# Attention with inducing points and a top-1 expert layer on one core: logits in column tiles, weights spread by a matmul, one gather per batch, and new numbers in the planner

## The chip, the cores and the metric

The kernel runs on one core of one Trainium2 chip. The metric is device time in microseconds (us): the median over runs of the program. The profile is of one execution.

## The reference, cut to what matters

```python
# x: (4, 11456, 128), inducing: (32, 128); 8 experts of width 1024; all fp32
def mab(q, kv):
    s = scale * (q @ kv.transpose(0, 2, 1)); s = s - s.max(-1, keepdims=True)
    a = np.exp(s); a /= a.sum(-1, keepdims=True) + 1e-09
    return a @ kv
h = mab(I, x)            # pass 1: 32 inducing points attend to 11456 rows
y = mab(x, h)            # pass 2: each row attends to the 32 rows of h
logits = y @ w_gate; expert_idx = np.argmax(logits, axis=1)
probs = softmax(logits); gate_w = probs[arange, expert_idx]
for e in range(E):       # the rows of expert e
    out[mask] = gate_w[mask, None] * (np.maximum(y[mask] @ w1[e], 0) @ w2[e])
```

## The kernel before, in words

Each of the four batches has six groups (24 in all), each of 4 segments by 15 blocks of 32 rows. A group's x lies in SBUF with channels on partitions (an xT tile, 0.98 MB); pass 1 needs it with rows on partitions as well: either loaded a second time (an xn load, 0.99 MB) or made on chip by 15 transposes on TensorE and four evictions (a group in `TURNED`). All big tiles (xT, xn and the output tiles ob) share 17 buffers; the 8 PSUM banks are shared too.

**Pass 1**, per group: scores S1 (`scores`, L445, four matmuls in four column tiles), maximum M1, exp E1, 32x32 block transposes T1, and the sum H (`h_sum`, L498). After six groups: the rows h, centred h (`h_center`), and `gate_mm`, `pick`: which expert all rows of the batch are expected to choose, from the mean of h. POOL then gathers the 128 rows of that expert's w1 (GA1) and of its w2 (GA2) by two indirect DMAs of 0.5 MB (`gather`, L549). From w1 come the hidden units G (`units`, L588, on TensorE), from those and w2 a 32x128 matrix h4 (`second`, L610, `part_fold`, L622), and a threshold (`extremes`, `margin`, `margin_all`, `threshold`) above which a row's choice is certain.

**Pass 2**, per group: scores S2 against centred h, M2 (`max2`), E2 (`exp2`). Then by rounds of one to four groups: LG (`logits`, L666), one 128x128 by 480 matmul for each group, all accumulating into one bank, where `gzb` puts group u's logits in its own columns; LV (`logits_turn`); the gate: RS, LS on POOL, PR on ACT, LM, GE, DN, C. C gives a weight for each row. For each group then CB (`spread`, L720, a DVE transpose that spreads the weights over the 32 points), W (`weigh`, L723, on POOL: e times cb), X (`experts`, L727, four matmuls in four row tiles, each to its own bank), four evictions V (L464 on ACT or L466 on DVE) into ob, and the store OUT (L439). At the end `count_left` (op LEFT) counts rows without a certain choice and, if there are any, a general part redoes them.

**The order** is made on the host by `schedule` (L59): it simulates the five engines with the planner's durations and due times, at each moment starts the ready op of lowest rank on each engine, and the instructions are written out in that order. On the chip each engine runs its own instructions strictly in that order, so an instruction whose input is late holds up all behind it. Ranks are `ONE`, `TWO` (a base and a step for each batch), `EARLY` for loads. A gather is planned to be done `GATHER` = 3600 ns after its 1100 ns issue:

```python
if o.dma:
    line = max(line, t + d + 500) + o.dma
    if e == "SP":
        o.end = line + LANDING
    ...
    else:
        o.end = t + d + GATHER
```

Of the kernel before, what the change touches and what calls it, by code (L numbers as in the profile page):

```python
# [18 lines left out]
P = 128  # L19
# [4 lines left out]
GB = 15  # L24
# [11 lines left out]
HOP, LANDING, INFLIGHT, GATHER, BEHIND = 70, 1400, 4, 3600, 450  # L36
# [21 lines left out]

def schedule(ops, caps, groups):  # L59
# [16 lines left out]
    line = inflight = t = done = 0  # L76

# [19 lines left out]
    while done < len(ops):  # L97
        for e in ENGINES:
# [25 lines left out]
            if o.dma:  # L124
                line = max(line, t + d + 500) + o.dma
                if e == "SP":
                    o.end = line + LANDING
                    inflight += 1
                    at(line, 1, o)
                else:  # L130
                    o.end = t + d + GATHER
# [25 lines left out]
D_S, D_H, D_X, D_LG, D_T4 = 830, 830, 860, 850, 440  # L157
PE_LAT = 180
# [9 lines left out]
ONE = ((-13.0, 0.5), (21.6, 0.8), (52.7, 3.0), (87.0, 3.4))  # L168
TWO = ((28.9, 6.3), (85.7, 4.0), (71.5, 10.3), (153.7, 6.2))
EARLY = 26.0  # L170
# [11 lines left out]
def make_plan(K):  # L182
# [3 lines left out]
    def op(name, rank, dur, fn, deps=(), take=(), use=(), lat=0, dma=0):  # L186
        if "PE" in dur and not lat:
            lat = PE_LAT
        o = Op(name, rank, dur, fn, deps, take, use, lat, dma)
        ops.append(o)  # L190
        return o

    prev_m = [None] * B
    xts, e2s = {}, {}
    chain = {}
    done_ops = []
    xt_free = {}
    for b in range(B):
# [5 lines left out]
        for g in range(NG):  # L204
# [4 lines left out]
            ld = op(f"LT{k}", r - EARLY, {"SP": 60}, lambda xt=xt[g], b=b, g=g: K.load_xt(xt, b, g), take=[xt[g]], dma=BYTES)  # L209
            xt_free[k] = ld  # L210
            fe = Buf("fe")
            s1[g] = op(f"S1.{k}", r, {"PE": D_S}, lambda fe=fe, xt=xt[g]: K.scores(fe, K.it_s, xt), [ld], take=[fe], use=[xt[g]])
            m1[g] = op(f"M1.{k}", r + 1, {"DVE": 625}, lambda fe=fe, b=b, g=g: K.max1(fe, b, g), [s1[g]], use=[fe])
            if g in TURNED[b]:
                xr = []
                on = op(f"ON{k}", r + .1, {"POOL": 125}, lambda xn=xn[g]: K.ones_col(xn), [ld], take=[xn[g]])
                for n, k0 in enumerate(range(0, GB, 4)):
                    m = min(4, GB - k0)
                    o = Buf("o")
                    tr = op(f"TR{k}.{n}", r + .2 + .2 * n, {"PE": 110 * m}, lambda o=o, xt=xt[g], k0=k0, m=m: K.turn(o, xt, k0, m), [ld, on], take=[o], use=[xt[g]])  # L220
                    w = m * 128
                    xr.append(op(f"TE{k}.{n}", r + .8 + .2 * n, {"ACT": 80 + int(.99 * w), "DVE": 75 + int(1.19 * w)}, lambda e, o=o, xn=xn[g], k0=k0, m=m: K.turn_out(e, o, xn, k0, m), [tr, on], use=[o, xn[g]]))
                xnr = xr
            else:
                xnr = [op(f"LN{k}", r - EARLY + 1, {"SP": 60}, lambda xn=xn[g], b=b, g=g: K.load_xn(xn, b, g), take=[xn[g]], dma=BYTES)]
            e1b, e1t = Buf("e1"), Buf("e1t")
            e1[g] = (fe, e1b, e1t, xnr)
            if g % 2:
                p = g // 2
                mi = Buf("mi")  # L230
                mq = op(f"MQ{b}.{p}", r + 1.5, {"DVE": 130}, lambda b=b, p=p: K.max_spread(b, p), [m1[g - 1], m1[g], nb_prev])
                fd = op(f"FD{b}.{p}", r + 1.6, {"PE": 220}, lambda mi=mi, b=b, p=p: K.max_fold(mi, b, p), [mq], take=[mi])
# [31 lines left out]
        gz = op(f"gz{b}", r + .5, {"DVE": 560}, lambda b=b: K.gate_cols(b), [a])  # L264
        gzb = op(f"gb{b}", r + .6, {"POOL": 1100}, lambda b=b: K.gate_block(b), [gz])
        m0 = Buf("mi")
        a = op(f"G{b}", r + 1, {"PE": 560}, lambda mi=m0, w=w, b=b: K.units(mi, w, b), [ga1, hT], take=[m0], use=[w])
        gt = op(f"GT{b}", r + 1, {"DVE": 440}, lambda mi=m0, b=b: K.units_turn(mi, b), [a], use=[m0])
        gs = op(f"GS{b}", r + 1, {"DVE": 420}, lambda b=b: K.units_sum(b), [gt])
        gl = op(f"GL{b}", r + 1, {"DVE": 600}, lambda b=b: K.units_keep(b), [gs])  # L270
        m0 = Buf("mi")
        a = op(f"P{b}", r + 1, {"PE": 560}, lambda mi=m0, w=w, b=b: K.second(mi, w, b), [gl, ga2], take=[m0], use=[w])
        a = op(f"PC{b}", r + 1, {"ACT": 280, "DVE": 280}, lambda e, mi=m0, b=b: K.part_out(e, mi, b), [a], use=[m0])
        m0 = Buf("mi")
        a = op(f"PF{b}", r + 1, {"PE": 360}, lambda mi=m0, b=b: K.part_fold(mi, b), [a], take=[m0])
        h4 = op(f"h4{b}", r + 1, {"ACT": 280, "DVE": 280}, lambda e, mi=m0, b=b: K.h4_out(e, mi, b), [a], use=[m0])
        a = op(f"dx{b}", r + 2, {"DVE": 840}, lambda b=b: K.extremes(b), [gl])
        a = op(f"dm{b}", r + 2, {"DVE": 1200}, lambda b=b: K.margin(b), [a])
        m0 = Buf("mi")
        a = op(f"DF{b}", r + 2, {"PE": 360}, lambda mi=m0, b=b: K.margin_all(mi, b), [a], take=[m0])  # L280
# [3 lines left out]
        for n in ROUNDS[b]:  # L284
            lg, lv, gate = Buf("mi"), Buf("lv"), Buf("gate")
            lgs = []
            rr = rank2(b * NG + g0 + n - 1)
            e2 = {}
            for u in range(n):
# [5 lines left out]
                s = op(f"S2.{k}", r, {"PE": D_S}, lambda fe=fe, xt=xt[g], b=b: K.scores(fe, K.hc[b], xt), [hc], take=[fe], use=[fe, xt[g]])  # L295
                mm = op(f"M2.{k}", r + 1, {"DVE": 780}, lambda fe=fe, k=k: K.max2(fe, k), [s], use=[fe])
                ex = op(f"E2.{k}", r + 2, {"ACT": 605}, lambda fe=fe, e=e2[u], k=k: K.exp2(fe, e, k), [mm], take=[e2[u]], use=[fe])
                lgs.append(op(f"LG{k}", rr + 2.7, {"PE": D_LG}, lambda lg=lg, e=e2[u], b=b, u=u, n=n: K.logits(lg, e, b, u, n), [ex, gzb, *lgs], take=[lg] if not u else [], use=[lg, e2[u]]))
            lt = op(f"LV{k}", rr + 3.6, {"DVE": 670}, lambda lg=lg, lv=lv: K.logits_turn(lg, lv), lgs[-1:], take=[lv], use=[lg])
            rs = op(f"RS{k}", rr + 3.7, {"DVE": 560}, lambda lv=lv, gt=gate, n=n: K.gate_rs(lv, gt, n), [lt], take=[gate], use=[lv])  # L300
            ls = op(f"LS{k}", rr + 3.8, {"POOL": 730}, lambda lv=lv, gt=gate, n=n: K.gate_ls(lv, gt, n), [rs], use=[lv, gate])
# [25 lines left out]
class Issue:  # L327
# [225 lines left out]
    def gather1(self, w, b):  # L553
        self.gather(self.w[w.slot][0], self.w1, b)
# [487 lines left out]
```

## Time and profile before

| | us |
|---|---|
| median of 3 runs | 205.47 (204.34 to 206.66) |
| profiled execution, its own time | 206.1 |
| its span, first to last instruction | 204.3 |
| busy PE / DVE / ACT / POOL | 162.1 / 132.0 / 95.9 / 56.9 |
| mean granted TensorE clock | 0.925 |
| bytes moved by DMA | 65.81 MB, 322 GB/s over the span |

PE is TensorE's matmuls, PEld its weight loads, DVE VectorE, ACT ScalarE, POOL GpSimd, SP the engine that issues loads and stores. Lines such as L588 are of the kernel before. A chain of waits is followed back from the last instruction: at each step to what released it. Granted clock is a share of full speed: TensorE has two levels, 2.4 and 1.2 GHz, so 0.5 is the lower one throughout.

### The profile page before, as it was taken

How to read it: one execution, taken by the hardware profiler on the slowest of the kernel's cores; microseconds unless marked ns; L12 is line 12 of the kernel's file. 1: busy time of each engine (PE TensorE's matmuls, PEld its weight loads, DVE VectorE, ACT ScalarE, POOL GpSimd, SP SyncE). 2: the span in 40 equal slices, each digit the busy share in tenths (PEclk: the TensorE clock that was granted, in tenths of full speed). 3: DMA queues.
4: the chain of work that ended last, by engine and by line, in shares of the span. 5: the costliest groups of instructions: out<-in, count | busy, mean ns of one | idle time of the engine just before them, and what ended most of it. 6: DMA issues, size and time to landing. Idle time of an engine off the chain costs nothing.

```text
span 204.3 us, 4408 instructions
## 1 busy us (share of the span) xinstructions
PE 162.1 (79%) x1664; PEld 83.3 (41%) x1665; DVE 132.0 (65%) x375; ACT 95.9 (47%) x197; POOL 56.9 (28%) x91
## 2 busy tenths in 40 slices
PE   0599999673999799379997999199999969983900
PEld 0274866353343357144224954026553223341300
DVE  1125737961579899746669889186998985997500
ACT  2056561071033663705635483307777725767630
POOL 0000000230003734710024635202373740397200
PEclk9999999996799999969999999969999988998585
DMA  6999999999997089999879899944058898179792
GB/s 206 419 423 424 415 424 409 423 408 421 413 410 290 3 262 365 397 423 390 316 311 349 308 418 348 415 178 189 6 241 325 288 374 332 75 313 385 290 404 94
DMA packets 10541, 65.81 MB, mean 322 GB/s; under 512 B 1424, under 2 KB 1552, under 8 KB 10512
## 3 DMA queue, kind: packets, MB, share of 16 engines
q1 hardware_dynamic: 8928, 61.06, 75.2%
q0 software_dynamic: 1152, 4.19, 5.6%
q8 instruction: 15, 0.25, 0.5%
q10 hardware_dynamic: 432, 0.20, 0.3%
q14 instruction: 14, 0.11, 0.2%
HBM read 41.85 MB, written 23.59 MB: 320 GB/s over the span
## 4 chain that ended last, share of the span: by engine, by line
PE 46%; DMA 21%; DVE 18%; ACT 4%; issue 3%; POOL 2%; ACTq 0%; DVEq 0%; POOLq 0%
DMA w1r<-in_w,ii 17%; PE bank L445 11%; PE bank L727 8%; PE bank L666 8%; PE bank L498 7%; PE bank L456 7%; DMA csb<-in_consts 4%; ACT big L464 2%; DVE e1t L488 2%; POOL e L723 2%; DVE mx L659 2%; PE bank L588 2%; DVE cb L720 2%; ACT e L485 1%; DVE mx L448 1%
## 5 line engine op out<-in xcount | busy, mean ns | idle before, releaser
L464 ACT COPY big<-bank 128x480 f32<-128x480 f32 (+2 forms) x121 | 60.4, 580 | 40.5 <-PE bank L727 22.8
L723 POOL TENSOR_TENSOR e<-e,cb 128x480 f32<-128x480 f32 x24 | 28.6, 1210 | 33.5 <-DVE cb L720 21.7
L727 PE MATMUL bank<-e,h 32*128 32x480 f32 x192 | 32.2, 691 | 1.9 <-POOL e L723 1.9
L445 PE MATMUL bank<-big,it_s 128*32 128x480 f32 x192 | 26.8, 615 | 6.4 <-DVE it_s L409 6.4
L498 PE MATMUL bank<-big,e1t 128*32 128x129 f32 x720 | 28.3, 287 | 1.9 <-DVE mq L471 1.6
L498 PEld LDWEIGHTS bank<-big,e1t 128*32 128x32 f32 x720 | 23.7, 115 | 10.1 <-issue 3.4
L663 ACT ACTIVATE e<-bank,nb 128x480 f32<-128x480 f32 x24 | 15.8, 671 | 24.2 <-DVE nb L660 12.0
L666 PE MATMUL bank<-e,gzb 128*128 128x480 f32 x48 | 26.7, 646 | 0.0
L445 PE MATMUL bank<-big,hc 128*32 128x480 f32 x192 | 25.7, 592 | 0.0
L448 DVE TENSOR_REDUCE mx<-bank 128x1 f32<-128x480 f32 x24 | 15.3, 643 | 11.3 <-PE bank L445 11.3
L456 PE MATMUL bank<-csb,big 128*128 128x128 f32 x150 | 20.4, 291 | 0.9 <-DMA csb<-in_consts 0.9
L686 POOL TENSOR_TENSOR ls<-lv,rs 128x315 f32<-128x315 f32 (+3 forms) x9 | 6.1, 678 | 53.4 <-DVE rs L683 48.8
L485 ACT ACTIVATE e<-bank,mx 128x480 f32<-128x480 f32 x24 | 14.9, 667 | 12.4 <-DVE mx L482 12.3
L456 PEld LDWEIGHTS bank<-csb,big 128*128 128x128 f32 x150 | 18.0, 151 | 6.3 <-DMA csb<-in_consts 2.5
L727 PEld LDWEIGHTS bank<-e,h 32*128 32x128 f32 x192 | 11.6, 208 | 15.3 <-issue 6.1
L488 DVE STREAM_TRANSPOSE e1t<-e 128x480 f32<-128x480 f32 x24 | 15.1, 653 | 2.0 <-ACT e L485 2.0
L659 DVE TENSOR_REDUCE mx<-bank 128x1 f32<-128x480 f32 x24 | 15.3, 638 | 1.3 <-PE bank L445 1.3
L720 DVE STREAM_TRANSPOSE cb<-c 128x480 f32<-128x480 f32 x24 | 15.3, 660 | 1.1 <-POOL e L723 0.9
L588 PE MATMUL bank<-w1r,hT_all 128*32 128x256 f32 x32 | 3.6, 523 | 15.1 <-DMA w1r<-in_w,ii 15.1
L466 DVE COPY big<-bank 128x480 f32<-128x480 f32 (+2 forms) x15 | 9.4, 627 | 8.8 <-PE bank L456 6.2
L666 PEld LDWEIGHTS bank<-e,gzb 128*128 128x128 f32 x48 | 7.9, 204 | 15.5 <-issue 10.8
L445 PEld LDWEIGHTS bank<-big,it_s 128*32 128x32 f32 x192 | 5.8, 113 | 14.0 <-DVE it_s L409 6.1
(94 smaller groups left out, 142.2 us busy)
## 6 DMA issues: line engine op xcount, KB each, us to landing
big<-in_xT SPq DMA_DIRECT2D x24, 960.0 KB, 11.6
out<-big SPq DMA_DIRECT2D x24, 960.0 KB, 4.8
big<-in_xn SPq DMA_DIRECT2D x14, 967.5 KB, 11.4
csb<-in_consts ACTq DMA_DIRECT2D x1, 172.5 KB, 7.9
w1r<-in_w,ii POOLq DMA_INDIRECT x4, 9.7
w2r<-in_w,ii POOLq DMA_INDIRECT x4, 9.9
it_s<-in_indT ACTq DMA_DIRECT2D x1, 16.0 KB, 5.4
wg_sb<-in_wg ACTq DMA_DIRECT2D x1, 4.0 KB, 9.8
```

What stands on the lines that cost most here:

```text
L445: self.nc.tensor.matmul(self.blk(ps[32 * q : 32 * q + 32, :GW]), lhsT=lhsT, rhs=x[:, :, q, :], start=True, stop=True)
L448: self.nc.vector.tensor_reduce(self.mx1[b][g // 2][:, g % 2 : g % 2 + 1], self.bank(fe)[:, :GW], AX.X, ALU.max)
L456: self.nc.tensor.transpose(ps[:, k * P : (k + 1) * P], x[:, k0 + k].rearrange("p q t -> p (q t)"), self.ident)
L464: self.nc.scalar.copy(dst, src)
L485: self.nc.scalar.activation(self.at(e), self.bank(fe)[:, :GW], AF.Exp, bias=self.mx1[b][p + 1][:, 2:3])
L488: self.nc.vector.transpose(self.at(t), self.at(e))
L498: self.nc.tensor.matmul(ps[32 * j : 32 * j + 32, : P + 1], lhsT=e[:, k, :], rhs=x[:, k, :], start=(n < 4), stop=(n >= 2 * GB - 4))
L659: self.nc.vector.tensor_reduce(t, self.bank(fe)[:, :GW], AX.X, ALU.max)
L666: self.nc.tensor.matmul(self.bank(lg)[:, :GW], lhsT=self.gzb[b][:, u].rearrange("p q s -> p (q s)"), rhs=self.at(e), start=(u == 0), stop= ...
L720: self.nc.vector.transpose(self.blk(self.at(cb)), c)
L723: self.nc.gpsimd.tensor_tensor(out=self.at(e), in0=self.at(e), in1=self.at(cb), op=ALU.mult)
L727: self.nc.tensor.matmul(self.bank(os_[q])[:, :GW], lhsT=self.h4[b][32 * q : 32 * q + 32, :], rhs=self.at(e)[32 * q : 32 * q + 32, :], star ...
```

## The change

- **Logits.** `gzb` shrinks from four 128x128 blocks to one 128x32 block. A round's LG is one op: n matmuls of 128x32, group u in column tile u, so the logits of group u stand on partitions 32u to 32u+31. All gate ops of a round work on 32n partitions and 60 columns instead of 128 partitions and 15n columns. LM, GE and DN go; C applies the threshold itself.
- **Weights.** Instead of a CB for each group: one DVE transpose CT (`gate_back`) for each round, then for each pair of groups SP (`spread`, "SEL" below): a matmul for each group, 32 rows of a 0/1 matrix `sel` against 480 columns, to a PSUM bank `cb`. W runs on DVE and reads that bank. `cb` buffers move from SBUF to the 8 shared banks.
- **Gather.** w1 and w2 lie side by side in one array `wcat`; one indirect DMA of 1 MB per batch replaces two.
- **Planner.** New durations; a gather is due 9030 ns after its start (1080+1500+700+2x2500+750) if the planned DMA line is busy, 6530 ns if not; a model of TensorE's clock; 8 planned loads in flight for 4; new ranks; `EARLY` 26 to 209.3. `ROUNDS` go from 9 to 10, turned groups from 10 to 9 (so one xn load more).
- **Smaller.** inducing points and constants are loaded on SP's queue, the latter behind the first xT; part of the threshold's work moves to POOL; `gate_mm` starts before centred h; the last two groups are stored in halves; LEFT reduces one array `c_all`.

```diff
-HOP, LANDING, INFLIGHT, GATHER, BEHIND = 70, 1400, 4, 3600, 450
+HOP, BEHIND = 55, 500
+FETCH, LANDING, INFLIGHT = 1500, 750, 8
[...]
...
+            if e == "PE":
+                d *= clock.speed(t)
+                clock.add(t, t + d)
...
-                line = max(line, t + d + 500) + o.dma
+                queued = line > t + d + FETCH
+                line = max(line, t + d + FETCH) + o.dma
...
-                    o.end = t + d + GATHER
+                    o.end = t + d + FETCH + 700 + (2 * o.dma if queued else o.dma) + LANDING
...
-TURNED = {0: (0, 1, 2, 3, 4), 1: (3,), 2: (3,), 3: (0, 1, 4)}
-
-ROUNDS = {0: (3, 3), 1: (4, 2), 2: (4, 2), 3: (3, 2, 1)}
-CAPS = {"e1": 3, "e1t": 4, "e2": 7, "cb": 2, "lv": 2, "gate": 2, "w": 1}
-GROUPS = {"bank": (8, {"fe": 3, "o": 5, "mi": 3}), "big": (17, {"xt": 10, "xn": 4, "ob": 4})}
...
+TURNED = {0: (0, 1, 2, 3, 5), 1: (3,), 2: (2,), 3: (0, 4)}
+
+ROUNDS = {0: (2, 2, 2), 1: (4, 2), 2: (2, 4), 3: (1, 4, 1)}
+
+HALVES = (22, 23)
+CAPS = {"e1": 3, "e1t": 4, "e2": 8, "lv": 3, "gate": 2, "w": 1}
+GROUPS = {"bank": (8, {"fe": 3, "o": 5, "mi": 3, "cb": 2}), "big": (17, {"xt": 10, "xn": 4, "ob": 4})}
...
-        ga1 = op(f"GA1.{b}", r, {"POOL": 1100}, lambda w=w, b=b: K.gather1(w, b), [a], take=[w], dma=1250)
-        ga2 = op(f"GA2.{b}", r, {"POOL": 1000}, lambda w=w, b=b: K.gather2(w, b), [a, ga1], use=[w], dma=1250)
...
+        ga = op(f"GA{b}", r, {"POOL": 1080}, lambda w=w, b=b: K.gather(w, b), [ix], take=[w], dma=2500)
...
+            a = op(f"C{k}", rr + 4.2, {"DVE": 1350}, lambda gt=gate, n=n, b=b, nr=nr: K.gate_c(gt, n, b, nr), [a, thr], use=[gate])
+            ct = op(f"CT{k}", rr + 4.3, {"DVE": 590}, lambda lv=lv, n=n, nr=nr: K.gate_back(lv, n, nr), [a], use=[lv])
+            rounds.append(ct)
+            for u0 in range(0, n, 2):
+                us = range(u0, min(u0 + 2, n))
+                cbs = [Buf("cb") for _ in us]
+                sp = op(f"SP{b * NG + g0 + u0}", rr + 4.4 + u0, {"PE": D["SEL"]}, lambda cbs=cbs, lv=lv, u0=u0: K.spread(cbs, lv, u0), [ct, sel], take=cbs, use=[lv])
+                for u, cb in zip(us, cbs):
...
+                    wg = op(f"W{k}", ru + .1, {"DVE": 650}, lambda cb=cb, e=e2[u]: K.weigh(cb, e), [sp], use=[cb, e2[u]])
...
+                    step = 2 if k in HALVES else 4
...
+    def logits(self, lg, es, b):
+        for u, e in enumerate(es):
+            self.nc.tensor.matmul(
+                self.bank(lg)[32 * u : 32 * u + 32, :GW], lhsT=self.gzb[b].rearrange("p q j -> p (q j)"), rhs=self.at(e), start=True, stop=True
+            )
...
+    def gate_back(self, lv, n, r):
+        self.nc.vector.transpose(self.lv4(lv, n), self.c_all[0 : 32 * n, r].unsqueeze(3).to_broadcast([32 * n, GB, NQ, E]))
+
+    def spread(self, cbs, lv, u0):
+        for i, cb in enumerate(cbs):
+            rows = slice(32 * (u0 + i), 32 * (u0 + i) + 32)
+            self.nc.tensor.matmul(
+                self.bank(cb)[:, :GW], lhsT=self.sel[rows].rearrange("p q m -> p (q m)"), rhs=self.at(lv)[rows], start=True, stop=True
+            )
...
-        self.nc.gpsimd.tensor_tensor(out=self.at(e), in0=self.at(e), in1=self.at(cb), op=ALU.mult)
+        self.nc.vector.tensor_tensor(out=self.at(e), in0=self.at(e), in1=self.bank(cb)[:, :GW], op=ALU.mult)
...
-        nc.vector.memset(self.done[64:128, :, NBLK - 1 : NBLK], 1.0)
-        nc.vector.tensor_scalar(self.left, self.done.rearrange("p b n -> p (b n)"), -1.0, 1.0, op0=ALU.mult, op1=ALU.add)
-        nc.vector.tensor_reduce(self.cnt, self.left, AX.X, ALU.add)
+        nc.vector.tensor_reduce(self.cnt[:, 0:1], self.c_all.rearrange("p r k q -> p (r k q)"), AX.X, ALU.min)
+        nc.vector.tensor_single_scalar(self.cnt[:, 1:2], self.cnt[:, 0:1], 0.0, op=ALU.is_le)
```

## Rows read from the trace of the kernel before

**Rows 1.** The profile's page: span, busy time by engine, and the span in 40 slices of 5.1 us (tenths of busy time, for PE and for the mean of the 16 DMA engines).

```profile
span 204.3 us, 4408 instructions
PE 162.1 (79%) x1664; PEld 83.3 (41%) x1665; DVE 132.0 (65%) x375; ACT 95.9 (47%) x197; POOL 56.9 (28%) x91
...
PE   0599999673999799379997999199999969983900
...
DMA  6999999999997089999879899944058898179792
```

**Rows 2.** The page's chain that ended last, by line, in shares of the span.

```profile
DMA w1r<-in_w,ii 17%; PE bank L445 11%; PE bank L727 8%; PE bank L666 8%; PE bank L498 7%; PE bank L456 7%; DMA csb<-in_consts 4%; ACT big L464 2%; DVE e1t L488 2%; POOL e L723 2%; DVE mx L659 2%; PE bank L588 2%; DVE cb L720 2%; ACT e L485 1%; DVE mx L448 1%
```

**Rows 3.** What TensorE's matmuls waited for, over the whole span: us in total, times, longest.

```profile
PE bank L588 <- DMA w1r<-in_w,ii: 15.1, 4, 4.7
PE bank L445 <- DVE it_s L409: 6.4, 1, 6.4
PE bank L744 <- DVE cnt L742: 3.6, 1, 3.6
PE bank L727 <- POOL e L723: 1.9, 2, 1.2
```

**Rows 4.** The chain in order of time (start, length): the four first gathers, from POOL's start to landing.

```profile
39.46 9.48 DMA w1r<-in_w,ii
...
78.37 9.85 DMA w1r<-in_w,ii
...
122.19 9.85 DMA w1r<-in_w,ii
...
158.83 6.06 DMA w1r<-in_w,ii
```

**Rows 5.** Stretches of the span: busy us of PE, PEld, DVE, ACT, POOL (with instructions), granted clock, DMA share, GB/s. The first four begin where G starts after its gather; the fifth is the end; the sixth holds half of the rounds.

```profile
49.00:56.00 7.00, 6.92 (x57) 3.35 (x58) 3.50 (x14) 0.00 (x0) 0.00 (x0) 0.64 1.02 417
88.30:92.40 4.10, 4.05 (x50) 2.57 (x54) 2.74 (x10) 0.00 (x0) 0.00 (x0) 0.60 1.01 423
132.10:136.30 4.20, 4.12 (x22) 1.21 (x22) 3.00 (x12) 0.00 (x0) 0.00 (x0) 0.59 0.69 286
165.00:170.30 5.30, 5.27 (x24) 1.50 (x25) 4.23 (x16) 1.75 (x4) 1.99 (x2) 0.68 0.95 363
184.00:194.20 10.20, 6.57 (x30) 2.42 (x26) 6.58 (x17) 6.82 (x16) 4.88 (x8) 0.67 0.84 344
140.00:190.00 50.00, 43.92 (x374) 19.49 (x376) 42.19 (x121) 32.08 (x70) 25.17 (x36) 0.94 0.68 267
```

**Rows 6.** The chain in order of time, whole ops of TensorE while the clock was at its upper level: 15 transposes of a group, two scores back to back, and one X, one group's LG, one scores (each logical fp32 matmul has two records).

```profile
13.78 1.79 PE bank L456 x15
...
92.39 1.75 PE bank L445 x16
...
98.38 1.02 PE bank L727 x8
99.39 1.00 PE bank L666 x2
100.40 0.94 PE bank L445 x8
```

**Rows 7.** Groups of instructions by shape (busy us, mean ns), and then, from the timeline (start, length), two gate ops of the last round, which has one group.

```profile
L723 POOL TENSOR_TENSOR e<-e,cb 128x480 f32<-128x480 f32 x24 | 28.6, 1210 | 33.5 <-DVE cb L720 21.7 <-ACT e L485 9.4 <-PE bank L727 2.2
L720 DVE STREAM_TRANSPOSE cb<-c 128x480 f32<-128x480 f32 x24 | 15.3, 660 | 1.1 <-POOL e L723 0.9
L466 DVE COPY big<-bank 128x480 f32<-128x480 f32 x10 | 6.5, 648 | 2.6 <-PE bank L727 2.4
L686 POOL TENSOR_TENSOR ls<-lv,rs 128x420 f32<-128x420 f32 x2 | 1.8, 922 | 19.2 <-DVE rs L683 19.2
L712 DVE TENSOR_REDUCE se<-ls 128x60 f32<-128x420 f32 x2 | 1.1, 564 | 0.0
L683 DVE RECIPROCAL rs<-sm 128x60 f32<-128x60 f32 x2 | 1.1, 528 | 0.1
...
184.08 0.38 POOL L686 TENSOR_TENSOR ls<-lv,rs 128x105 f32<-128x105 f32 x1
...
189.31 0.25 DVE L714 RECIPROCAL se<-se 128x15 f32<-128x15 f32 x1
```

**Rows 8.** The third batch's two gathers on POOL's timeline (start, length of the issue), and the page's line for the second gathers (median us from issue to landing).

```profile
122.19 1.06 POOL L549 DMA_INDIRECT w1r<-in_w,ii  x1 [2.46 <-DVE m L563]
...
124.49 0.99 POOL L549 DMA_INDIRECT w2r<-in_w,ii  x1 [0.16 <-issue]
...
w2r<-in_w,ii POOLq DMA_INDIRECT x4, 9.9
```

**Rows 9.** The end: the chain in order of time (start, length), and the last wait of SP's queue.

```profile
186.61 0.84 DVE left L741
187.47 0.54 DVE cnt L742
...
188.14 0.56 PE bank L744 x2
188.70 5.27 PE bank L727 x23
...
SPq L1037 <- DMA out<-big: 4.9, 1, 4.9
```

More of the change, by code (lines that the diff above doesn't have):

```diff
@@ L56, in __init__, with speed, add @@
             b.users += 1
+class Clock:
+    def __init__(self):
+        self.busy, self.fast = {}, {0: True}
+    def speed(self, t):
+        w = max(0, (t - PHASE) // WINDOW + 1)
+        for i in range(max(self.fast) + 1, w + 1):
+            self.fast[i] = self.busy.get(i - 1, 0) >= AWAKE[0 if self.fast[i - 1] else 1] * WINDOW
+        return 1 if self.fast[w] else 2
+    def add(self, t, end):
+        while t < end:
+            w = max(0, (t - PHASE) // WINDOW + 1)
+            stop = min(end, PHASE + w * WINDOW)
+            self.busy[w] = self.busy.get(w, 0) + stop - t
+            t = stop
 def schedule(ops, caps, groups):
@@ L76, in schedule @@
     line = inflight = t = done = 0
+    clock = Clock()
     def at(when, what, o):
@@ L184, in make_plan, with op @@
     ops = []
-    def op(name, rank, dur, fn, deps=(), take=(), use=(), lat=0, dma=0):
-        if "PE" in dur and not lat:
-            lat = PE_LAT
+    def op(name, rank, dur, fn, deps=(), take=(), use=(), lat=None, dma=0):
+        if lat is None:
+            lat = LAT.get(next(iter(dur)), 0)
         o = Op(name, rank, dur, fn, deps, take, use, lat, dma)
@@ L191, in op @@
         return o
[L193 to L197, printed above, removed]
+    xts, rounds = {}, []
+    it = op("IT", -1000, {"SP": 400}, lambda: K.load_it(), dma=60)
+    it = op("IS", -1000, {"DVE": 100}, lambda: K.scale_it(), [it])
+    cs = op("CS", rank1(0, 0) - EARLY + .01, {"SP": 400}, lambda: K.load_consts(), dma=500)
+    sel = op("SL", 20, {"POOL": 300}, lambda: K.make_sel(), [cs])
     for b in range(B):
@@ L294, in make_plan @@
                 e2[u] = Buf("e2")
[L295 to L298, printed above, removed]
@@ L308, in make_plan @@
[L308 to L320 removed]
+                s = op(f"S2.{k}", r, {"PE": D["S"]}, lambda fe=fe, xt=xt[g], b=b: K.scores(fe, K.hc[b], xt), [hc], take=[fe], use=[fe, xt[g]])
@@ new lines, in make_plan @@
+                mm = op(f"M2.{k}", r + 1, {"DVE": 800}, lambda fe=fe, k=k: K.max2(fe, k), [s], use=[fe])
+                exs.append(op(f"E2.{k}", r + 2, {"ACT": 550}, lambda fe=fe, e=e2[u], k=k: K.exp2(fe, e, k), [mm], take=[e2[u]], use=[fe]))
+            es = [e2[u] for u in range(n)]
+            a = op(f"LG{k}", rr + 2.7, {"PE": D["LG"]}, lambda lg=lg, es=es, b=b: K.logits(lg, es, b), [gzb, *exs], take=[lg], use=[lg, *es])
+            a = op(f"LV{k}", rr + 3.6, {"DVE": 600}, lambda lg=lg, lv=lv, n=n: K.logits_turn(lg, lv, n), [a], take=[lv], use=[lg])
@@ new lines, in make_plan @@
+            a = op(f"RS{k}", rr + 3.7, {"DVE": 700}, lambda lv=lv, gt=gate, n=n: K.gate_rs(lv, gt, n), [a], take=[gate], use=[lv])
+            a = op(f"LS{k}", rr + 3.8, {"POOL": 920}, lambda lv=lv, gt=gate, n=n: K.gate_ls(lv, gt, n), [a], use=[lv, gate])
+            a = op(f"PR{k}", rr + 3.9, {"ACT": 480}, lambda gt=gate, n=n: K.gate_exp(gt, n), [a], use=[gate])
+            a = op(f"C{k}", rr + 4.2, {"DVE": 1350}, lambda gt=gate, n=n, b=b, nr=nr: K.gate_c(gt, n, b, nr), [a, thr], use=[gate])
@@ L321, in make_plan @@
             g0 += n
     m0 = Buf("mi")
-    op("LEFT", 1e3, {"DVE": 1800}, lambda: K.count_left(m0), done_ops, take=[m0])
+    op("LEFT", 1e3, {"DVE": 900}, lambda: K.count_left(m0), rounds, take=[m0])
     return ops
@@ L350, in __init__ @@
         self.hT = new("hT_all", [P, B, P])
-        self.done = new("done_all", [P, B, NBLK])
-        self.left = new("left", [P, B * NBLK])
-        self.cnt = new("cnt", [P, 1])
+        self.rounds = sum(map(len, ROUNDS.values()))
+        self.c_all = new("c_all", [P, self.rounds, GB, NQ])
+        self.cnt = new("cnt", [P, 2])
         self.nleft = new("nleft", [P, 1], I32)
-        self.load = [lambda: nc.scalar.dma_start(self.it_s, indT), lambda: nc.scalar.dma_start(csb, consts), lambda: nc.scalar.dma_start(self.wg, wg)]
         self.pool = pool
@@ L759, in attn_moe_kernel @@
                 o.fn()
-    general_part(tc, K, xT, wg, w1, w2, out)
+    general_part(tc, K, xT, wg, wcat, out)
 def blk(t):
```

363 lines of the change are left out of this document (185 added, 178 removed).

## The prediction, made before the change was run

> **What bounds the kernel now.** I read the page first, then TensorE's waits, then the chain in order of time, and last the stretches that the chain points at. The page shows two resources that are near full for long stretches and neither over the whole span: PE is busy 162.1 of 204.3 us, the DMA engines are full to about 60 us and then in pieces [rows 1]. 65.81 MB at the 417 to 423 GB/s of a full stretch [rows 5] would take 157 us. So neither a byte nor a matmul count sets the time; what sets it is where PE stands still. The chain says where: its largest entry is the first gather of each batch, 17% of the span [rows 2], and PE waited 15.1 us for it in four waits [rows 3]. The reader should see that this is an error of order, not lack of work. The plan of before has the gather done 1100+3600 = 4700 ns after its start, so G is written into PE's order there; three gathers took 9.48 to 9.85 us and one 6.06 [rows 4]. The differences, 4.8, 5.2, 5.2 and 1.4, are 16.6 us, and PE waited 15.1. Behind each G stood work that doesn't need the gather: PE is 98% busy right after it [rows 5]. And the wait is paid twice, since the clock drops after it: granted 0.64, 0.60, 0.59 and 0.68 over the 7.0, 4.1, 4.2 and 5.3 us that follow [rows 5]. (1 - clock) x length gives 2.5+1.6+1.7+1.7 = 7.6 us lost. The fourth place is the end: PE waits 3.6 us for LEFT's reduction [rows 3, 9], the clock is 0.67 in that stretch [rows 5], and the last X follow it.
>
> **The change part by part**, against the profiled execution's 206.1 us (1.8 more than its span, 0.6 over the median of the runs).
>
> *Gather.* One of 1 MB instead of two of 0.5 MB. No row has one of 1 MB. Bounds from rows: the first half alone, 9.85 us after POOL's start, and both halves: the second is issued 2.3 us later and lands 9.9 after that, 12.2 in all [rows 4, 8]. Below the first half nothing can be excluded where the queue is short (6.06 in the fourth batch). Two halves in flight together each took as long as either, so I take a value near the lower end, 10.3 us. The new plan has it due at 9.03 us. Residual wait 1.3 us a batch, 5 in all, for 15.1: **-10**; with both ends +0.8 to 3.2 a batch, -12 to -2.
>
> The gather shares the DMA engines with SP's loads. In three batches with full DMA the first half took 9.5 to 9.85 us, in the fourth 6.06 [rows 4]. The Trainium skill, page "DMA: Bandwidth & Descriptors", section "Queues, rings and completion order", says that each DMA engine takes turns between the queues it has work for, packet by packet, so a queue of POOL's need not wait for all of SP's. By that rule twice as many planned loads in flight would cost the gather nothing; read as one line instead, it would land behind them. The trace, with 9.5 to 9.85 whenever the queue was full, doesn't tell the two apart. The second reading is a rival below.
>
> *Clock after those waits.* 7.6 us lost; with waits of 1.3 for 4.5 us I let 5 of it come back: **-5** (0 to -7.6).
>
> *PE's work.* LG: 24 times 1.00 = 24.0 us become 10 ops. Four scores in column tiles take 0.94 us against 1.00 for one full matmul, so 10 x 0.94 = 9.4: -14.6 [rows 6]. SEL is added: 4+2, 2+4, 2+2+2 and 1+4+1 groups give 13 pairs or singles. The nearest row is X, four row tiles in 1.02 us [rows 6]; a pass of two tiles costs at least half of that and at most the same, if the two run beside each other, so 0.51 to 1.02; I take 1.02: +13.3. One turned group less: -1.8 [rows 6]. Sum **-3** (-10 to -3, and to +10 if a pair ran one after the other). PE is the engine in whose order the waits stand, so I count this in full.
>
> SEL has another tile shape than scores and H. Two scores back to back take 1.75 us, one between other shapes 0.94, so a change of shape shows as 0.07 us [rows 6]. The Trainium skill, page "TensorEngine Tiling (Array Packing)", section "Key Properties", says that changing the tiling mode drains TensorE, which speaks against 13 more visits of another shape. The 1.02 of X already holds such a change; by the rule alone two for each SEL would add 26 x 0.07 = 1.8 us, by the row nothing more, and LG, now of the same shape as scores, gives some back.
>
> *Weigh and spread.* W on POOL took 1.21 us, CB on DVE 0.66 [rows 7]. W on DVE from a bank is not in the trace; the nearest row is DVE's copy of the same size from a bank, 0.65 [rows 7], and it cannot be shorter than that pass by much or longer than POOL's 1.21; I take 0.65. So 24 W replace 24 CB on DVE at no cost. Added: 10 CT at 0.66 = 6.6. The gates of all rounds have 60 columns: with a tenth round +2, and what goes with LM about pays for the wider ops. DVE 132 to about 140 us. Over 140 to 190 us DVE is busy 42.2 of 50 [rows 5], and five of the ten rounds end there, so it would come to about 46.5; most hides in its gaps: **+2** (0 to +8). What hides it is DVE's idle 3.5 us in that stretch; with that gone all 4.3 show.
>
> *New waits.* SEL waits on PE for CT, with scores, H and X of other groups queued behind it; W waits on DVE for SEL, with maxima and transposes behind it; X waits for W. Before, X waited 1.9 us for POOL in two places [rows 3]. I take the same again: 0 (up to 13 x 0.3 = +4). POOL loses its 24 W, so nothing stands ahead of a gather or of LS; the threshold's two visits to POOL lie beside E2 and LG of the round: 0, and 1 us a batch if not hidden. The banks for cb are paid for by LG's, held for one op instead of up to four: 0.
>
> *End.* LEFT's two DVE ops, 0.84 and 0.54, become one reduction over 600 columns, an estimate of 0.8 from 0.65 for 480 [rows 7, 9], and a short one; the plan still books PE's matmul inside a DVE op: **-2.5** of 3.6. The last round has one group, but its gate ops now have the 60 columns: the two reciprocals 0.53 for 0.25 each (+0.56), LS 0.92 for 0.38 (+0.54), and by the same proportion an estimated 0.3 each for the sum and for ACT's exponential; CT, SEL and W take 2.33 where CB and W took 1.87 (+0.46) [rows 6, 7]. Together **+2.2**. The last store is half as large: 0.98 MB at 420 GB/s is 2.3 us, half of it **-1** of the 4.9 us wait [rows 9].
>
> *Start.* Constants come behind one xT instead of beside six on another queue; S1 begins at 6.4 us as before [rows 3], the transposes behind it a little earlier: **-1** (0 to -2). The extra xn load is 2.35 us of DMA time; the DMA engines are far from full after 60 us [rows 1]: 0, at most +2.35.
>
> Sum: -10 - 5 - 3 + 2 - 2.5 + 2.2 - 1 - 1 = -18.3, so 187.8 for the profiled execution and **187** with the 0.6 to the median taken off.
>
> **The rivals.**
>
> *Better: the order holds.* If G comes after the landing everywhere, both gather terms go in full (-22.7 for -15) and the SEL pairs take the lower end (-10 for -3 at the best, half of it here): 187 - 8 - 3.5 = 175.5, call it **176**. A floor for it: 162.1 - 7.6 - 3 = 151.5 us of PE work, 6.4 before the first matmul and 10 from the last one to the end is 168. For: PE never lacked work behind a G. Against: the 42 us that PE idled are not all gathers.
>
> *DVE takes over.* If DVE's extra 8 us are all on the path and each W delays its X, +6 and +4 on the forecast: **197**. For: 84% busy over 140 to 190 [rows 5], and W now stands in DVE's order. Against: over the span it is 65% [rows 1].
>
> *SEL pairs don't overlap* (the change doesn't do what it says): 11 pairs at 2.04 add 11 us: **198**. Against: X's four tiles, to four banks, take 1.02 [rows 6].
>
> *Slower: the gather lands behind SP's line.* With loads ranked ahead of all else and eight planned in flight, 8 x 2.34 us could stand ahead of a merged gather. PE waits at G for 4 x (landing - 9.03). With the clock loss staying, the rest of the sum is -3.3, so the break-even is 15.1 + 3.3 = 18.4 of waits, a landing of 13.6 us. At 16 us: 28 of waits, 206.1 - 3.3 + 12.9 = 215.7, **215** on the median. For: the landing tracks how full the DMA is [rows 4]. Against: it stayed below 9.9 with 417 GB/s moving beside it.
>
> **How the numbers follow.** Chances: forecast 0.53, better 0.16, DVE 0.12, SEL 0.04, gains that reappear as other waits so that nothing is left (205, within 1%) 0.06, slower 0.09. About 1% is what a measurement of this kernel can tell from no change, its three runs lying within 0.6% of their median. Faster: 0.53+0.16+0.12+0.04 = 0.85. The range 175 to 200 takes in the forecast with its bounds, the DVE and SEL cases and most of the better one, and leaves out 0.15 and the tails.
>
> **What would show it.** Right: G waits for its gather under 2 us a time; the granted clock after G stays above 0.9; LG 0.94 a round and SEL about 1.0 a pair; W 0.65; PE's wait for LEFT about 1 us. Wrong: gathers landing past 12 us; W waited for by PE for more than 5 us in all; DVE over 90% in the last third; or PE idle with its next op waiting for loads, which would mean that the shared big tiles, not the gathers, held it.

## The result and the profile after

The changed kernel takes 187.9 us (median of 4, 184.6 to 189.7) where the kernel before took 205.5; the ratio is 0.905 [0.891, 0.919]. Run unaltered two more times beside the experiments it gave 0.911 [0.907, 0.916] and 0.932 [0.921, 0.943], so these three differ by up to 3%. Ratios throughout leave out disturbed runs, which medians contain; where the two disagree the ratio is the one to use. The profiled execution took 187.3 us, its span 185.4.

The page of the kernel after, to be laid beside [rows 1]: span, busy time, the slices of PE, of the granted clock and of the DMA engines, and the line of the merged gather (median us from issue to landing).

```profile
span 185.4 us, 4365 instructions
PE 154.0 (83%) x1697; PEld 79.0 (43%) x1698; DVE 127.3 (69%) x348; ACT 100.3 (54%) x206; POOL 20.0 (11%) x50
...
PE   0698999799884999999999996999999598689700
...
PEclk9999999999996599999999999999999999756955
DMA  5999999999999949999999999991969957945993
...
wr<-in_wcat,ii POOLq DMA_INDIRECT x4, 10.4
```

Of the 18.9 us that the span lost, PE's busy time gave 8.1 (162.1 to 154.0) and its idle time 10.8 (42.2 to 31.4). What TensorE waited for, over the whole span (us in total, times, longest; L630 is G, L767 SEL, L776 X, L490 scores), against [rows 3]:

```profile
PE bank L490 <- DMA big<-in_xT: 7.1, 2, 6.3
PE bank L630 <- DMA wr<-in_wcat,ii: 3.8, 3, 2.1
PE bank L767 <- DVE lv L762: 3.7, 2, 2.5
PE bank L776 <- DVE e L772: 1.1, 1, 1.1
```

The gather's 15.1 us have become 3.8. LEFT's 3.6 are gone from the list: its matmul now waits 0.4 us. Of the new waits only SEL's, 3.7 us for CT, is of any size. The chain in order of time, three of the four gathers (the longest is among them), with the G that follows (start, length), against [rows 4]:

```profile
36.61 10.42 DMA wr<-in_wcat,ii
...
47.07 0.68 PE bank L630 x8
...
101.51 10.56 DMA wr<-in_wcat,ii
...
138.65 8.41 DMA wr<-in_wcat,ii
...
147.19 0.64 PE bank L630 x8
```

G takes 0.64 to 0.68 us each time; before it took 1.08, 1.08, 0.77 and 0.64. In this execution the clock did not fall at any G. Stretches of the kernel after, in the columns of [rows 5]: the first two start at a G, then one place in the middle, then the end.

```profile
47.00:52.00 5.00, 4.58 (x53) 1.69 (x54) 4.50 (x12) 1.48 (x3) 1.75 (x4) 1.00 1.01 416
...
112.00:117.00 5.00, 4.25 (x33) 1.84 (x34) 3.85 (x13) 3.43 (x7) 0.49 (x2) 1.00 1.02 424
...
55.00:65.00 10.00, 7.48 (x78) 4.07 (x76) 7.54 (x18) 1.95 (x4) 0.51 (x3) 0.66 1.02 423
...
156.00:170.00 14.00, 10.81 (x44) 4.24 (x43) 10.24 (x23) 8.53 (x20) 0.91 (x1) 0.64 0.62 257
170.00:182.00 12.00, 4.63 (x27) 2.27 (x26) 1.10 (x4) 6.59 (x14) 0.00 (x0) 0.78 0.96 384
```

After all four G the granted clock is 1.00 for 5 us, but two new stretches at 0.66 and 0.64 have come, one behind PE's idle while DVE works through the first gates, one at the end; there X takes 1.99 us instead of 1.02. In the last 12 us of these the DMA engines are full with stores. In a later execution of the changed kernel, unaltered (190.5 us), the fourth G did lose the clock, behind a wait of 1.8 us: the timeline, and the stretch around it.

```profile
149.06 1.08 PE L630 MATMUL bank<-wr,hT_all 128*32 128x256 f32 x8 [1.80 <-DMA wr<-in_wcat,ii]
...
148.00:153.00 5.00, 3.94 (x24) 1.52 (x28) 3.06 (x9) 2.03 (x5) 0.38 (x2) 0.66 0.73 304
```

The prices that the prediction had to guess, as the trace after has them (busy us, mean ns), and three whole TensorE ops from its chain (start, length):

```profile
L772 DVE TENSOR_TENSOR e<-e,bank 128x480 f32<-128x480 f32 x24 | 14.9, 643 | 4.6 <-PE bank L767 4.5
L762 DVE STREAM_TRANSPOSE lv<-c_all 64x480 f32<-64x480 f32 x5 | 3.2, 650 | 0.0
L511 DVE COPY big<-bank 128x480 f32<-128x480 f32 (+1 forms) x3 | 2.0, 660 | 0.8 <-PE bank L501 0.8
...
73.11 1.00 PE bank L767 x4
...
83.85 1.75 PE bank L490 x16
...
86.03 0.81 PE bank L720 x8
```

W 0.643, CT 0.65, a SEL pair 1.00 at the upper clock (1.97 at the lower), a round's LG of four groups 0.81 us, 0.85 and 0.94 in the other two such rounds. DVE makes three evictions where it made 15.

### The profile page after: what moved, and what is told of

Read it like the earlier page. It is cut to its first block, busy times and chain, and to the rows that moved or that the text cites. A ratio compares the mean times of both kernels' runs of the same rounds, so it can differ in the third digit from the quotient of the medians.

```text
span 185.4 us, 4365 instructions
## 1 busy us (share of the span) xinstructions
PE 154.0 (83%) x1697; PEld 79.0 (43%) x1698; DVE 127.3 (69%) x348; ACT 100.3 (54%) x206; POOL 20.0 (11%) x50
## 4 chain that ended last, share of the span: by engine, by line
PE 49%; DMA 24%; DVE 11%; ACT 6%; issue 3%; SPq 2%; ACTq 0%; DVEq 0%
DMA wr<-in_wcat,ii 16%; PE bank L490 13%; PE bank L776 10%; PE bank L543 9%; DMA big<-in_xT 7%; PE bank L501 6%; ACT big L509 5%; PE bank L767 4%; DMA out<-big 2%; DVE mx L493 1%; PE bank L630 1%; PE bank L720 1%; SPq L478 1%; DVE lv L725 1%; DVE e L772 1%
## 5 line engine op out<-in xcount | busy, mean ns | idle before, releaser
L509 ACT COPY big<-bank 128x480 f32<-128x480 f32 (+2 forms) x129 | 63.8, 582 | 30.5 <-PE bank L776 15.4
L776 PE MATMUL bank<-e,h 32*128 32x480 f32 x192 | 33.8, 664 | 1.9 <-DVE e L772 1.1
L490 PE MATMUL bank<-big,it_s 128*32 128x480 f32 x192 | 27.3, 610 | 7.4 <-DMA big<-in_xT 7.1
L490 PE MATMUL bank<-big,hc 128*32 128x480 f32 x192 | 26.7, 573 | 0.7 <-ACT e L716 0.5
L530 ACT ACTIVATE e<-bank,mx 128x480 f32<-128x480 f32 x24 | 14.8, 666 | 17.8 <-DVE mx L527 17.6
L767 PE MATMUL bank<-lv,sel 32*128 32x480 f32 x48 | 17.2, 729 | 3.7 <-DVE lv L762 3.7
L776 PEld LDWEIGHTS bank<-e,h 32*128 32x128 f32 x192 | 12.5, 199 | 16.9 <-issue 7.1
L772 DVE TENSOR_TENSOR e<-e,bank 128x480 f32<-128x480 f32 x24 | 14.9, 643 | 4.6 <-PE bank L767 4.5
L501 PE MATMUL bank<-csb,big 128*128 128x128 f32 x135 | 18.0, 284 | 0.0
L501 PEld LDWEIGHTS bank<-csb,big 128*128 128x128 f32 x135 | 15.4, 146 | 5.7 <-issue 4.9
L740 POOL TENSOR_TENSOR ls<-lv,rs 64x420 f32<-64x420 f32 (+2 forms) x10 | 9.1, 915 | 50.7 <-DVE rs L737 30.4
L490 PEld LDWEIGHTS bank<-big,it_s 128*32 128x32 f32 x192 | 5.1, 111 | 13.0 <-issue 9.0
L749 ACT ACTIVATE ls<-ls 64x420 f32<-64x420 f32 (+2 forms) x10 | 5.6, 560 | 8.0 <-POOL ls L740 8.0
L720 PE MATMUL bank<-e,gzb 128*32 128x480 f32 x48 | 9.8, 569 | 0.1
L767 PEld LDWEIGHTS bank<-lv,sel 32*128 32x128 f32 x48 | 5.7, 223 | 9.2 <-ACT big L509 2.9
L490 PEld LDWEIGHTS bank<-big,hc 128*32 128x32 f32 x192 | 5.7, 108 | 8.5 <-issue 3.4
## 6 DMA issues: line engine op xcount, KB each, us to landing
big<-in_xT SPq DMA_DIRECT2D x24, 960.0 KB, 14.4
big<-in_xn SPq DMA_DIRECT2D x15, 967.5 KB, 16.2
wr<-in_wcat,ii POOLq DMA_INDIRECT x4, 10.4
```

Source lines behind the costliest of these rows:

```text
L490: self.nc.tensor.matmul(self.blk(ps[32 * q : 32 * q + 32, :GW]), lhsT=lhsT, rhs=x[:, :, q, :], start=True, stop=True)
L501: self.nc.tensor.transpose(ps[:, k * P : (k + 1) * P], x[:, k0 + k].rearrange("p q t -> p (q t)"), self.ident)
L509: self.nc.scalar.copy(dst, src)
L530: self.nc.scalar.activation(self.at(e), self.bank(fe)[:, :GW], AF.Exp, bias=self.mx1[b][p + 1][:, 2:3])
L767: self.nc.tensor.matmul(self.bank(cb)[:, :GW], lhsT=self.sel[rows].rearrange("p q m -> p (q m)"), rhs=self.at(lv)[rows], start=True, stop=True
L772: self.nc.vector.tensor_tensor(out=self.at(e), in0=self.at(e), in1=self.bank(cb)[:, :GW], op=ALU.mult)
```

## The experiments

All experiments on the changed kernel keep its written order of instructions, unless said otherwise: the planner runs unaltered, and the ops are altered afterwards.

### The due time alone, in the kernel before

```diff
+def replan(K):
+    global GATHER
+    place = {o.name: i for i, o in enumerate(schedule(make_plan(K), CAPS, GROUPS))}
+    ops = make_plan(K)
+    for o in ops:
+        o.rank = place[o.name]
+    GATHER = 8750
+    return schedule(ops, CAPS, GROUPS)
...
-        for o in schedule(make_plan(K), CAPS, GROUPS):
+        for o in replan(K):
```

> The kernel before with one number of its plan changed: a gather is due 8750 ns after its issue instead of 3600, so that G comes later in TensorE's order; all other ranks are the places of the ops in the order of before. Theory (the gather's due time is the main term): G waits for under 2 us in all instead of 15.1, the clock after G stays above 0.9, and the time falls by 12 to 20 us, to 186 to 194. Rival (the gain came from the cheaper logits, the weigh off POOL and the rest of the plan): less than 6 us, above 200.

192.4 us, ratio 0.944 [0.936, 0.952]: -12.6 us by the medians on this chip, -11.5 by the ratio, at the low end of the theory's range or just under it. What TensorE waited for longest:

```profile
PE bank L445 <- DVE it_s L409: 6.2, 1, 6.2
PE bank L744 <- DVE cnt L742: 3.4, 1, 3.4
PE bank L727 <- POOL e L723: 3.4, 3, 1.9
```

G's wait for its gather, 15.1 us in [rows 3], is no longer among these, and the clock rose from 0.925 to 0.953. PE's busy time fell from 162.1 to 155.9 us and its idle time from 42.2 to 34.1. No operation was made cheaper here, though with the one number the whole order was planned anew (the second gather, for one, was issued 8.4 us behind the first in the second batch). By the ratios this is 60% of the change, 0.056 of 0.095, and more by the other two ratios of the changed kernel. No run splits the rest, at most 8 us, between the logits, the weights and the other new numbers of the planner.

### The old due time put back into the kernel after

```diff
+            i = next(i for i, x in enumerate(order) if x.eng == "PE" and x.start >= o.start + 1080 + 3600)
...
+            fn = lambda w=o.take[0], b=b, slot=slot: K.look(w, b, slot)
+            extra.append((i, Op(f"LOOK{b}", 0, {"PE": 0}, fn)))
...
+    def look(self, w, b, slot):
+        w1 = self.w[w.slot][:, 0:F].rearrange("c (f j t) -> c j f t", j=4, t=32)
+        self.nc.tensor.matmul(
+            self.banks[slot][0:32, 0:256].rearrange("p (f t) -> p f t", t=32), lhsT=self.hT[:, b, 0:M], rhs=w1[:, 0], start=True, stop=True
+        )
```

> The changed kernel, same order, with one matmul more for each batch that reads the gathered w1, put into TensorE's order where the old plan had the gather due (4680 ns after its start). Its result isn't used. Theory: TensorE waits there 10.4 - 4.7 = 5.7 us for three gathers and 3.7 for the fourth, 21 us for the 3.8 of now, and loses some clock after it: 187.9 + 17 + 4 to 7, 203 to 212. Rival (the waits lie beside DVE's work and the evictions, which set the time anyway): under 194.

212.8 us, ratio 1.042 [1.032, 1.052]: all of the change is lost and more, a little above the theory's range. TensorE's waits at the added matmul (L636), and the run's span and clock:

```profile
PE bank L636 <- DMA wr<-in_wcat,ii: 14.7, 3, 5.6
...
core 0: 211.2 us, clock 0.882
```

Three waits of about 5 us, as in [rows 3], and a fourth place of 3.9 us that the profile puts down to ACT; there the added matmul starts 8.35 us after its gather, about the 8.4 us of that landing, so it is the gather's as well. 14.7+3.9 for 3.8 is 14.8 us of waits more. The span grew by 25.8 us: PE's idle time by 14.1 (31.4 to 45.5) and its busy time by 11.7 (154.0 to 165.7). Of the 11.7 most is the clock: busy time times (1 - clock), summed over stretches of 1 us, rises from 7.5 to 17.0, 9.5 more; what is left goes to the added matmuls. So a wait on TensorE costs here about 1.6 times its length, the part above one through the clock. Before, it was 1.5 times: 15.1 us of waits and 7.6 us of clock behind them [rows 3, 5].

### Two gathers instead of the merged one

```diff
-        self.nc.gpsimd.indirect_dma_start(
-            out=self.w[w.slot], out_offset=None, in_=self.wcat, in_offset=bass.IndirectOffsetOnAxis(ap=self.ii[b % 2][:, :1], axis=0)
-        )
+        for dst, src in zip(self.w[w.slot], (self.w1, self.w2)):
+            self.nc.gpsimd.indirect_dma_start(
+                out=dst, out_offset=None, in_=src, in_offset=bass.IndirectOffsetOnAxis(ap=self.ii[b % 2][:, :1], axis=0)
+            )
```

> The changed kernel, same order, with each merged gather issued as two of 0.5 MB back to back, into two tiles. Theory (merging is worth little): first half lands 9.5 to 10 us after the start, G waits as now, 187 to 190. Rival (merging itself gained, by one issue less and an earlier w2): 191 or more.

182.7 us, ratio 0.897 [0.889, 0.906]: neither expectation; it is faster than the changed kernel. To see whether that was the chip, both were run once more side by side.

> The changed kernel, unaltered, for comparison on the same chip: 185 to 189.

> Two gathers of 0.5 MB back to back once more, beside the unaltered kernel. Theory (w1 alone lands 1.6 us earlier than the merged 1 MB, so the 3.8 us that TensorE still waits at G go, with some clock behind them): 2 to 5 us less than the unaltered one. Rival (the 182.7 was that chip): within 1 us of it.

Merged: 190.6 us, ratio 0.932 [0.921, 0.943], its lowest run 188.2. Two gathers: 182.9, ratio 0.900 [0.891, 0.910], its highest run 184.3. The intervals don't meet, and the highest run of the one is 3.9 us below the lowest of the other: two gathers are some 7 us faster on this chip, more than the theory had. On another chip, with ten evictions moved in both (below), it is 0.902 for 0.915, some 2.5 us. So the sign holds, and the size goes with the chip. Their page's lines for the two halves:

```profile
w1r<-in_w,ii POOLq DMA_INDIRECT x4, 9.2
w2r<-in_w,ii POOLq DMA_INDIRECT x4, 11.6
```

Each is counted from its own issue. w1 alone lands 1.2 us earlier than the merged 10.4; w2, issued 1.3 us behind it, lands 12.9 us after the start of the pair, 2.5 later than the merged one, while its first user comes well behind G and waited 0.9 us once. G no longer waits for its gather (3.0 us in the merged run beside it), and on the same chip the later gathers start earlier by 3.7, 4.2 and 5.1 us from batch to batch (70.2, 99.5 and 135.8 us for 73.9, 103.7 and 140.8). Not all of that is G's wait: of the 8.8 us between the two spans (188.7 and 179.9) PE's busy time makes 7.2. The merged run has four stretches at the lower clock before PE's last matmul and lost 10.9 us of busy time in them, the other two stretches and 3.4 us; only one of the four, the one shown above, lies behind a G. What the split did for the others isn't shown.

### Double the selection matmuls

```diff
+            for _ in range(2):
+                self.nc.tensor.matmul(
+                    self.bank(cb)[:, :GW], lhsT=self.sel[rows].rearrange("p q m -> p (q m)"), rhs=self.at(lv)[rows], start=True, stop=True
+                )
```

> The changed kernel, same order, with each selection matmul issued twice to the same bank: 13 passes of 1.0 us more on TensorE that the plan doesn't know. Theory (TensorE's work counts in full, as the sum took it): +10 to +14, 198 to 202. Rival (it hides in TensorE's idle 31 us): under +5, below 193.

190.2 to 196.0 us in four runs, median 193.9. The unaltered kernel wasn't run on this chip. The two lower runs are 0.93 and 0.94 of the kernel before beside them, and the unaltered kernel had 0.905 to 0.932 elsewhere: the cost is somewhere between 0 and 7 us. The full price of +10 to +14 is out; the rival, under +5, isn't. The work added was also less than 13 us, some 10, since a doubled pair takes 1.82 us where a pair takes 1.00 (start, length):

```profile
73.98 1.82 PE bank L768 x8
```

In the profiled execution, the lowest of the four, PE's busy time is 6.4 us above the unaltered 154.0, and the busy time lost to the lower clock is 3.1 us for 7.5, so part of the added work came back there through the clock (0.961 for 0.931 over the span). Two of the four runs had 0.925 and nothing of the kind.

### Double the weighs on VectorE

```diff
+        self.nc.vector.tensor_tensor(out=self.twice, in0=self.at(e), in1=self.bank(cb)[:, :GW], op=ALU.mult)
         self.nc.vector.tensor_tensor(out=self.at(e), in0=self.at(e), in1=self.bank(cb)[:, :GW], op=ALU.mult)
```

> The changed kernel, same order, with each weigh on VectorE done twice, the first time into a tile that nothing reads: 24 x 0.65 = 15.5 us more on VectorE. Theory (VectorE is beside TensorE's path for most of the span): +4 to +8. Rival (VectorE has become the bound): +12 to +16. If it hides wholly: under +3.

195.7 us, ratio 0.956 [0.950, 0.961], beside 0.911 of the unaltered kernel on the same chip:

> The changed kernel again, unaltered, for comparison on the same chip: 184 to 190.

That one gave 188.5 (185.7 to 193.2). The difference of the ratios is 0.045, 9 us, give or take 1.5, for 15 us of added work. So some 60% of work added at the weighs shows in the time, at the upper end of the theory or just above it, and less than the rival's 12. What the rest of VectorE's work is worth was not tried.

### Evictions at the end, and the clock at the end

```diff
+LATE = [f"V{k}.{q}" for k, q in ((18, 3), (19, 3), (20, 1), (20, 3), (21, 1), (21, 3), (22, 1), (22, 3), (23, 1), (23, 3))]
...
+            if o.name in LATE:
+                o.eng = "DVE"
```

> The changed kernel, same order; of the 24 evictions of the last six groups, all on ScalarE, ten go to VectorE, which is 90% idle after 170 us. Theory (the end waits for evictions, 24 x 0.49 us in a row on one engine): 2 to 4 us less than the unaltered one. Rival (the X before them, at the lower clock, or VectorE's weighs behind these copies set the end): within 1 us of it, or slower.

189.5 us, ratio 0.915 [0.909, 0.920], the same as the unaltered 0.911.

> Two gathers of 0.5 MB back to back, and the ten evictions on VectorE. If what two gathers gave in the earlier run (182.7) is no accident of that chip, and the end waits for evictions: 178 to 181. If two gathers give nothing against the unaltered kernel on the same chip: 183 or more.

184.6 us, ratio 0.902 [0.898, 0.907]: under the 0.915 of the same evictions with the merged gather, so two gathers hold on a second chip with both beside each other, but no better than two gathers alone (0.897 and 0.900 elsewhere). Its last 8 us before the final store lands:

```profile
170.00:175.00 5.00, 0.09 (x1) 0.00 (x0) 1.22 (x3) 0.16 (x1) 0.00 (x0) 0.69 1.00 401
175.00:178.00 3.00, 0.00 (x0) 0.00 (x0) 0.00 (x0) 0.00 (x0) 0.00 (x0) 0.50 1.01 388
```

All evictions are done by about 171 us, and the DMA engines are full to 178 with the stores that are left. From TensorE's last matmul to the end of the span it is 12.0 us here and 11.7 with the merged gather; without the moved evictions 10.9 and 10.4. So the ten evictions on VectorE brought nothing, and the stretch behind the last X grew by about 1 us. In the unaltered kernel the chain runs through two X at the lower clock, and then ScalarE's last evictions wait for a store to free an output tile (start, length).

```profile
160.33 1.99 PE bank L776 x8
...
164.71 1.99 PE bank L776 x8
...
168.65 3.73 DMA out<-big
...
172.40 2.88 ACT big L509 x6
```

The last version raises the clock there, with matmuls that nothing reads:

```diff
+FILL = {"SP18": 6, "X18": 6, "SP19": 4, "SP21": 4}
...
+    def fill(self, slot, n):
+        for _ in range(n):
+            self.nc.tensor.matmul(self.banks[slot][:, 0:P], lhsT=self.ones, rhs=self.h4[2], start=True, stop=True)
```

> Two gathers, and 20 matmuls of 128x128 by 128 into free banks, whose results nothing reads, written into TensorE's order ahead of four late ops where it stood idle (SEL of groups 18, 19 and 21, X of group 18). Theory (the lower clock from 156 to 170 us delays the X of the last batch and so its stores): clock at the upper level there, 1 to 3 us less than two gathers alone. Rival (the line of the last six stores, 14 us of DMA time, sets the end from its first store on): within 1 us, or slower by the added matmuls.

184.3 us, ratio 0.903 [0.896, 0.910]: the time is the rival's. The clock is at the upper level from 155 to 170 us, as meant,

```profile
155.00:160.00 5.00, 5.00 (x36) 3.35 (x35) 3.50 (x9) 1.99 (x5) 0.91 (x1) 1.00 0.92 381
160.00:165.00 5.00, 4.17 (x32) 2.28 (x33) 3.37 (x7) 3.38 (x8) 0.00 (x0) 1.00 0.49 200
```

and it brings nothing. That doesn't show that the clock is worth nothing there. The added matmuls take 5.5 us of PE's time themselves, more than the 1.7 and 3.0 us of busy time that the two runs of two gathers alone lost to the lower clock near the end. The last X of each run from TensorE's timeline (start, length; 24 records are three X), in the order unaltered (span 185.4), two gathers on the first chip (180.6), on the second (179.9), and with the added matmuls (183.0):

```profile
170.84 4.17 PE L776 MATMUL bank<-e,h 32*128 32x480 f32 x24
...
165.48 4.17 PE L777 MATMUL bank<-e,h 32*128 32x480 f32 x24
...
164.22 4.78 PE L777 MATMUL bank<-e,h 32*128 32x480 f32 x24
...
168.01 4.17 PE L781 MATMUL bank<-e,h 32*128 32x480 f32 x24
```

With the added matmuls these X end 34.9 us after the last gather starts, without them 33.6 and 33.2. And in all four the span ends 10.4 to 10.9 us after them, so the end still moves with TensorE. The two runs of two gathers can't price the clock either: one has 0.56 and the other 0.96 from 160 to 165 us with spans only 0.7 us apart, but the lower stretch of the second lies at 164 to 168 instead. What the clock near the end is worth stays open.

### LEFT last, in the kernel before with the later due time

```diff
+        order = replan(K)
+        order.sort(key=lambda o: o.name == "LEFT")
+        for o in order:
```

> The kernel before with the later gather due time (as in the earlier run, 192.4) and LEFT written last in the order. Theory (LEFT's wait of 3.4 us on TensorE delays the last X): 2 to 3 us under 192.4. Rival (evictions and stores set the end): within 1 us of it.

190.4 us, ratio 0.934 [0.925, 0.944], on another chip than the 192.4 (0.944 [0.936, 0.952]). The wait of 3.4 us left the list of TensorE's waits; the 2 us agree with the theory, but the intervals overlap, so it isn't shown by itself.

## Why the prediction was right

**The gather's due time** carried it, as the sum had it (-10 and -5 of -18.3). The landing was taken as 10.3 us and is 10.4 (8.4 in the last batch); the residual wait as 5 us and is 3.8. The runs show the cause from both sides: the due time alone gives -12.6 in the kernel before, the old due time put back costs +25 in the kernel after. The slower rival needed landings past 13.6 us; the longest in the changed kernel is 10.6, with the DMA engines full. It is out: the loads of xT and xn took 14.4 and 16.2 us from issue to landing for 11.6 and 11.4 before, and a gather of twice the size hardly more than before, so it did not stand behind their line.

**The clock** was right in place and only about half right in size. In the profiled execution all 7.6 us after the gathers came back, not 5; but TensorE stands idle elsewhere now, and its lower clock moved there. Busy time times (1 - clock), summed over 1 us stretches, is 10.4 us before and 7.5 after: 2.9 net. The execution of 190.5 us lost 10.9, no less than before, so this term comes and goes from run to run. What the stretch at the end is worth stays open; of the one at 55 to 65 us nothing was tried.

**TensorE's work.** SEL at 1.00 us a pair (taken as 1.02) is as priced, LG at 0.81 to 0.94 for four groups (0.94) as priced or cheaper, and the rival of pairs one after the other is out. Of the 8.1 us that PE's busy time lost, 2.9 are the clock, so 5.2 are work, where the sum had 3. Whether this work counts in full isn't settled: doubled SEL cost 0 to 7 us of some 10, so its full price is out for work added there.

**New waits** were taken as 0, with up to +4. SEL waits 3.7 us for CT, so it is the upper bound that came. X waits no longer than before.

**VectorE.** W was taken as 0.65 and is 0.643. The step that failed is the total: 132 to about 140 us was forecast, 127.3 came. The sum left out that the new plan gives VectorE 3 evictions where it had 15, 7.4 us of its busy time, and ScalarE 129 copies for 121. What that load is worth in time no run shows, so the +2 can't be checked; the rival built on it had the right engine, since 9 of 15 added us show, but not its load.

**The end.** LEFT's wait fell by 3.2 us, 2.5 were taken. The longer gates of the last round, +2.2, and the half stores, -1, can't be read from these runs. The sum didn't have the line of the last six groups' stores, 6 x 2.34 = 14 us at the DMA's rate. That more evictions on VectorE gave nothing and that the DMA engines are full to the end speak for it as a bound; no run moved the line itself, and the 10.4 to 10.9 us from TensorE's last matmul to the end speak for X as what starts its last part.

**The start.** The first scores wait 6.3 us for the first xT, 6.4 for the inducing points before, as forecast; PE is busy 3.7 us of the first 10 for 2.7, which fits the -1. The first gather starts 2.9 us earlier (36.6 for 39.5), so pass 1 of the first batch gained more than that; no run says by what. The extra xn load was taken as free because the DMA engines were "far from full after 60 us", which misreads [rows 1]: from 71 to 133 us they stand at 7 to 9 tenths. No run prices that load.

**One gather per batch** was priced only through its landing, and the row of the first half alone (9.85 us) stood in the sum as a bound, not as an alternative. The runs show it as a loss inside the change: with two gathers the same order takes 183 us, 2 to 7 less by chip. Issued back to back, the first half lands 9.2 us after the start and the second 12.9; the merged one, 10.4, lies between. G needs the first half only and no longer waits; the user of the second gains nothing that shows. How a wait of 3 to 4 us makes up to 7 is only in part accounted for, by the clock.

The 187 thus came out so near the 187.9 by luck as well, with errors that cancel. In the profiled spans the waits at G gave 11.3 us for 10, LEFT 3.2 for 2.5 and TensorE's work 5.2 for 3; the clock gave 2.9 for 5, and the new waits took 3.7 for 0. These five make up the 18.9 us; what the remaining terms of the sum did cancels or hides among them.

## What to carry to other kernels

Where the order is fixed ahead, compare a transfer's due time in the plan with its landing in the trace first: here that one number was worth more than everything else in the change. Count a wait on TensorE more than once, for itself and for the clock behind it: here it was 1.5 to 1.6 times. Try two transfers in place of a merged one when the first consumer needs only one of them. At the end of a kernel look for the line of stores before speeding up what fills it, and before judging filler by the clock that it keeps up, count the time that it takes itself.

## What had not been expected of the hardware

A wait of 5 us on TensorE cost about 8: 14.8 us of added waits came with 9.5 us of busy time lost to the lower clock, in a span 25.8 us longer. And in two of four runs some 10 us of added matmuls went with a mean clock of 0.956 and 0.961, above all sixteen runs of the unaltered kernel (0.896 to 0.947, on other chips as far as recorded), so that work put into idle stretches of TensorE can in part be paid back; the other two runs, at 0.925, show that it need not be. Two gathers of 0.5 MB issued back to back (9.2 and 12.9 us from the start of the pair) bring the half that is needed first earlier than one of 1 MB (10.4 us).
